# Writing down the order of ScalarE and VectorE, with weight slices between evacuations, in a retention and feed-forward kernel

## The chip, the cores and the metric

The kernel runs on one core of a Trainium2 chip. The metric is the device time of one execution in microseconds (us), as a median of several. Before the change it was 657.52 us (3 runs, 657.5 to 659.73). A difference counts as real here from 2% on; smaller ones are told with their intervals. All runs in this text are correct and in the fast state.

## The reference, cut to what matters

```python
# q, k, v: (4, 8, 768, 64) float32; w_in: 512 x 2048; w_out: 2048 x 512, both float64 by promotion
for t in range(S):                                     # retention, one state per head
    state = gamma * state + outer(k[t], v[t])
    y[t] = scale * q[t] @ state
x = y.transpose(0, 2, 1, 3).reshape(3072, 512)
h = x @ w_in                                           # 3072 x 2048
g = h * (1 / (1 + exp(-h)))                            # silu
return (g @ w_out).astype(float32)                     # 3072 x 512
```

## The kernel before

The sequence is cut into six chunks of 128 steps. A chunk c and a batch b make a *unit*, 24 in all; the four units of a chunk make *group* c, whose 512 rows of x go through w_in in 16 *products* (c, f), f being a slice of 128 columns. One unit's piece of attention is a *visit* (3.1 us of TensorE). When all 96 products are done, an output phase multiplies the stored g by w_out, a chunk of four output blocks at a time.

The weights arrive as float64. `convert_w` makes float32 out of them, one slice at a time, with one ScalarE operation (the absolute value `ca`) and six VectorE operations, the first two of them a sign and a clamp. `split_w` then makes three parts of the slice for three matrix passes. It is a chain across two engines: ScalarE high, VectorE low, then ScalarE middle and VectorE third.

```python
def split_w(f, w32, name, factor):
    w = w_slot(f, name)
    lo = conv.tile([128, 512], FP32, tag="wl", name=f"{name}l_{f}")
    with tc.issue_after(held[0] if f >= NF - 4 else evac[0]):
        nc.scalar.activation(out=w[:, 0, :], in_=w32, func=AF.Copy, scale=HALF * factor)
    high = w[:, 0, :].bitcast(FP32)
    nc.vector.scalar_tensor_tensor(out=lo, in0=w32, scalar=factor, in1=high, ...)
    nc.scalar.activation(out=w[:, 1, :], in_=lo, func=AF.Copy, scale=1.0 / EPS)
    nc.vector.scalar_tensor_tensor(out=w[:, 2, :], in0=high, scalar=EPS, in1=lo, ...)
    return w
```

A product is 12 matmuls into two of three banks (tiles of PSUM, the memory that TensorE writes), then an evacuation on ScalarE (a copy out of the first bank), a subtraction on VectorE (called g below; it reads the second bank) and the silu on ScalarE:

```python
def product_in(c, f):
    ha, hb = turn(f"ha_{c}_{f}"), turn(f"hb_{c}_{f}")          # two of three banks
    for i in range(3):
        for kk in range(KIN):
            nc.tensor.matmul(hb if i == 2 else ha, lhsT=w_sb[f][:, i, ts(kk, 128)], ...)
    nc.scalar.activation(out=hs, in_=ha, func=AF.Copy, scale=ONE_E)
    taken_out[:] = [nc.vector.tensor_tensor(out=hs, in0=hs, in1=hb, op=ALU.subtract).ins]
    nc.scalar.activation(out=hs, in_=hs, func=AF.Silu)
```

The order of TensorE is as written: after the first visits come eight products of two groups by turns (the *pairs*), twelve of three groups (the *threes*), then (2, 4) to (2, 11) and the rest. That of ScalarE and VectorE is the scheduler's, helped by `issue_after`:

```python
ctx.enter_context(tc.manual_schedule(engines={mybir.EngineType.PE}))
```

Group 2's x first lies in the place of the last four slices of w_in. It is therefore also stored, and read back into another place (`late_x`, the *readback*) before the products (2, 12) to (2, 15). g here and below is also the name of a product's result, the silu of h. The output phase ends each chunk with four blocks, in both kernels in the same words:

```python
for b in range(B):
    ...
    nc.scalar.activation(out=o, in_=oa, func=AF.Copy, scale=ONE_E)
    nc.vector.tensor_tensor(out=o, in0=o, in1=ob, op=ALU.subtract)
    nc.scalar.dma_start(out=out[ds(b * S + c * C, C), :], in_=o)
```

## Time and profile before

| Quantity | Before |
|---|---|
| Time | 657.52 us |
| Span in the profile | 655.4 us |
| TensorE (PE) busy | 617.1 us, 94% |
| VectorE (DVE) busy | 428.5 us, 65% |
| ScalarE (ACT) busy | 288.1 us, 44% |
| Last product done | about 388 us |

TensorE is the bound over the whole: 94% of the span. The two dearest groups of matmuls of the products, in the list of costliest groups, show it (line, engine, operation, tiles, shapes and count; then busy us and the mean ns of one; then idle time of the engine before them and what ended most of it):

```profile
L485 PE MATMUL ha<-xt,wi 128*128 128x512 f32 x768 | 194.2, 395 | 6.0 <-DVE g L490 4.3
L485 PE MATMUL hb<-xt,wi 128*128 128x512 f32 x384 | 103.0, 390 | 1.2 <-ACT g L489 1.1
```

In front of these 1152 matmuls there are 7.2 us of idle time in all: 4.3 us waiting for VectorE's subtraction g, 1.1 us for ScalarE's evacuation.

### The profile page before, as it was taken

The numbers are of one execution on the slowest core, as the hardware profiler recorded it, in microseconds if no ns is written. First come the engines' busy times: TensorE is split into PE (matmuls) and PEld (weight loads), VectorE is DVE, ScalarE is ACT, GpSimd is POOL, SyncE is SP. The second block draws the span as 40 slices with busy tenths as digits, with TensorE's granted clock in tenths as the row PEclk, the third lists the DMA queues.
The fourth block names the chain that finished last, engine by engine and source line by source line (L and its number), as shares of the span: only waits on it lengthen the run. The fifth ranks groups of instructions, "written<-read, shape, count | busy, mean of one in ns | idle before, by whom it ended". The sixth has DMA issues, their size and how long they took to land.

```text
span 655.4 us, 13531 instructions
## 1 busy us (share of the span) xinstructions
PE 617.1 (94%) x5440; PEld 509.2 (78%) x5440; DVE 428.5 (65%) x736; ACT 288.1 (44%) x522; POOL 14.9 (2%) x94
## 2 busy tenths in 40 slices
PE   4788889999999899999989999999999999999996
PEld 3676777888877687888768888888888888888885
DVE  2898989967968867658948856545463645454631
ACT  4546566756645444454437972222231412222311
POOL 3100000000000000000000000000000000000000
PEclk9998989999999999999999999999999999999999
DMA  9996775553577866767736654343242433433301
GB/s 196 211 209 153 198 199 179 185 171 127 192 242 170 235 178 162 226 170 237 240 113 225 202 169 127 100 159 101 92 163 95 147 110 98 159 99 95 129 0 64
DMA packets 123070, 103.64 MB, mean 158 GB/s; under 512 B 80000, under 2 KB 88192, under 8 KB 123008
## 3 DMA queue, kind: packets, MB, share of 16 engines
q1 hardware_dynamic: 119552, 96.49, 50.9%
q10 hardware_dynamic: 3456, 6.29, 2.6%
q8 instruction: 42, 0.69, 0.5%
q14 instruction: 20, 0.16, 0.1%
HBM read 66.06 MB, written 36.70 MB: 157 GB/s over the span
## 4 chain that ended last, share of the span: by engine, by line
PE 70%; DVE 17%; ACT 4%; DMA 3%; issue 3%; SPq 2%; ACTq 0%; DVEq 0%; POOL 0%; POOLq 0%
PE ha L485 18%; PE hb L485 9%; PE ob L612 7%; PE o L610 7%; PE oa L610 7%; PE o L611 7%; PE o L612 7%; PE oa L611 7%; SPq L144 2%; DVE cp L203 2%; DVE g L490 2%; DVE xt L433 2%; DVE cs L199 2%; PE y L387 1%; DVE am L363 1%
## 5 line engine op out<-in xcount | busy, mean ns | idle before, releaser
L485 PE MATMUL ha<-xt,wi 128*128 128x512 f32 x768 | 194.2, 395 | 6.0 <-DVE g L490 4.3
L485 PEld LDWEIGHTS ha<-xt,wi 128*128 128x128 f32 x768 | 142.6, 188 | 40.3 <-DVE g L490 8.3
L536 DVE TENSOR_TENSOR gs<-gr,gs 128x512 fp32r<-128x512 f32 x96 | 62.1, 685 | 90.3 <-ACT gs L534 90.3
L534 ACT ACTIVATE gs<-gr 128x512 fp32r<-128x512 f32 x96 | 53.5, 621 | 134.2 <-issue 131.8
L485 PE MATMUL hb<-xt,wi 128*128 128x512 f32 x384 | 103.0, 390 | 1.2 <-ACT g L489 1.1
L491 ACT ACTIVATE g<-g 128x512 f32<-128x512 f32 x96 | 60.6, 631 | 78.4 <-DVE g L490 78.2
L490 DVE TENSOR_TENSOR g<-g,hb 128x512 f32<-128x512 f32 x96 | 65.5, 682 | 44.4 <-PE hb L485 33.8
L485 PEld LDWEIGHTS hb<-xt,wi 128*128 128x128 f32 x384 | 71.9, 188 | 17.1 <-ACT g L489 1.6
L612 PE MATMUL ob<-wo,gs 128*128 128x512 f32 x192 | 75.3, 392 | 0.0
L610 PE MATMUL o<-wo,gs 128*128 128x512 f32 x192 | 74.7, 389 | 0.0
L610 PE MATMUL oa<-wo,gs 128*128 128x512 f32 x192 | 74.7, 389 | 0.0
L611 PE MATMUL o<-wo,gs 128*128 128x512 f32 x192 | 74.7, 389 | 0.0
L612 PE MATMUL o<-wo,gs 128*128 128x512 f32 x192 | 74.7, 389 | 0.0
L611 PE MATMUL oa<-wo,gs 128*128 128x512 f32 x192 | 74.7, 389 | 0.0
L489 ACT ACTIVATE g<-ha 128x512 f32<-128x512 f32 x96 | 56.6, 590 | 24.9 <-PE ha L485 20.1
L537 DVE SCALAR_TENSOR_TENSOR gs<-gs 128x512 fp32r<-128x512 f32 x96 | 61.9, 682 | 0.0
L612 PEld LDWEIGHTS ob<-wo,gs 128*128 128x128 f32 x192 | 36.0, 188 | 8.8 <-DVE o L618 1.5
L611 PEld LDWEIGHTS o<-wo,gs 128*128 128x128 f32 x192 | 36.0, 188 | 7.5
L612 PEld LDWEIGHTS o<-wo,gs 128*128 128x128 f32 x192 | 36.0, 188 | 7.5
L610 PEld LDWEIGHTS oa<-wo,gs 128*128 128x128 f32 x192 | 36.0, 188 | 7.5
L611 PEld LDWEIGHTS oa<-wo,gs 128*128 128x128 f32 x192 | 36.0, 188 | 7.5
L610 PEld LDWEIGHTS o<-wo,gs 128*128 128x128 f32 x192 | 36.0, 188 | 7.3
(80 smaller groups left out, 653.7 us busy)
## 6 DMA issues: line engine op xcount, KB each, us to landing
gd<-g SPq DMA_DIRECT2D x96, 256.0 KB, 2.9
gr<-gd SPq DMA_DIRECT2D x96, 256.0 KB, 2.7
wf<-in_moe_w_out_dram SPq DMA_DIRECT2D x16, 512.0 KB, 4.2
out_dram<-o ACTq DMA_DIRECT2D x24, 256.0 KB, 2.1
wf<-in_moe_w_in_dram SPq DMA_DIRECT2D x16, 256.0 KB, 3.2
wf<-in_moe_w_in_dram SPq DMA_DIRECT2D x32, 128.0 KB, 3.8
kf<-in_k_dram SPq DMA_DIRECT2D x16, 256.0 KB, 5.1
qf<-in_q_dram SPq DMA_DIRECT2D x16, 256.0 KB, 4.4
```

Of the source, the lines that this page charges most:

```text
L144: nc.sync.dma_start(out=t, in_=src[b, :, ds(c * C, C)].rearrange("h t d -> t h d"))
L199: nc.vector.scalar_tensor_tensor(out=s, in0=a, scalar=3, in1=s, op0=ALU.logical_shift_left, op1=ALU.bitwise_or)
L485: nc.tensor.matmul(hb if i == 2 else ha, lhsT=w_sb[f][:, i, ts(kk, 128)], rhs=xt[c][:, i, kk, :], start=kk == 0 and i != 1, stop=kk == KIN ...
L489: nc.scalar.activation(out=hs, in_=ha, func=AF.Copy, scale=ONE_E)
L490: taken_out[:] = [nc.vector.tensor_tensor(out=hs, in0=hs, in1=hb, op=ALU.subtract).ins]
L491: nc.scalar.activation(out=hs, in_=hs, func=AF.Silu)
L534: nc.scalar.activation(out=t[:, 0, :], in_=g, func=AF.Copy, scale=HALF)
L536: nc.vector.tensor_tensor(out=t[:, 1, :], in0=g, in1=high, op=ALU.subtract)
L537: nc.vector.scalar_tensor_tensor(out=t[:, 2, :], in0=t[:, 1, :].bitcast(FP32), scalar=-1.0 / EPS, in1=high, op0=ALU.mult, op1=ALU.add)
L610: nc.tensor.matmul(oa, lhsT=gh, rhs=wo[f][:, 0, :], start=first_, stop=False)
L611: nc.tensor.matmul(oa, lhsT=glo, rhs=wo[f][:, 1, :], start=False, stop=last)
L612: nc.tensor.matmul(ob, lhsT=gm, rhs=wo[f][:, 2, :], start=first_, stop=last)
```

## The change

Its intent is to take the order of ScalarE and VectorE from the scheduler and write it down: the conversion of weights becomes a generator that hands out single operations, and about 2000 ns of them are put in front of each product's evacuation, so that VectorE is always busy while TensorE multiplies. Two products, (1, 10) and (1, 11), are also moved behind (0, 12) to (0, 15), so that six products and not four are left to cover the readback of group 2's x. The diff, cut to its core ("..." marks cuts, here and below; comments in the diffs are added):

```diff
-    def split_w(f, w32, name, factor):
+    LONG, SHORT = 600, 360
+    def split_w(f, w32, name, factor, between=()):
         w = w_slot(f, name)
+        nc.scalar.activation(out=w[:, 0, :], in_=w32, func=AF.Copy, scale=HALF * factor)
+        yield from between                      # the next slice's absolute value, sign, clamp
         lo = conv.tile([128, 512], FP32, tag="wl", name=f"{name}l_{f}")
-        with tc.issue_after(held[0] if f >= NF - 4 else evac[0]):
-            nc.scalar.activation(out=w[:, 0, :], in_=w32, func=AF.Copy, scale=HALF * factor)
 ...
+        yield LONG
         nc.scalar.activation(out=w[:, 1, :], in_=lo, func=AF.Copy, scale=1.0 / EPS)
 ...
+    def fill(time):
+        while fillers and time > 0:
+            cost = next(fillers[0], None)
 ...
+                time -= cost
 ...
-    def product_in(c, f):
+    def product_in(c, f, time):
+        need(f + 1)
 ...
+        fill(time - catch_up())
         nc.scalar.activation(out=hs, in_=ha, func=AF.Copy, scale=ONE_E)
-        taken_out[:] = [nc.vector.tensor_tensor(out=hs, in0=hs, in1=hb, op=ALU.subtract).ins]
+        nc.vector.tensor_tensor(out=hs, in0=hs, in1=hb, op=ALU.subtract)
 ...
-    ctx.enter_context(tc.manual_schedule(engines={mybir.EngineType.PE}))
+    ctx.enter_context(tc.manual_schedule(engines={E.PE, E.Activation, E.DVE}))
 ...
+    half, full = NF // 2, 2000
 ...
+    steps += [(0, f) for f in early_f] + [(1, f) for f in early_f[:2]]
+    steps += [(0, f) for f in late_f] + [(1, f) for f in early_f[2:]]
 ...
+    here = steps.index((1, early_f[2]))
+    loads_at = {steps[here + b]: b for b in range(B)}
+    splits_at = {steps[here + 1 + b]: b for b in range(B)}
 ...
             if f < NF - 4:
-                w_out(f)
+                fillers.append(w_out(f))        # in group 5: before the evacuation, not after
+        product_in(c, f, full)
```

## The prediction

> **What bounds the kernel now.** I first cut the span where the program changes its work, with the view that sums each engine's busy time over stretches. Columns: stretch, its length, then busy time and instruction count of TensorE, weight load, VectorE, ScalarE, GpSimd, then granted clock, DMA share, GB/s.
>
> ```profile
> 55.00:104.00 49.00, 43.33 (x668) 36.06 (x665) 44.46 (x82) 28.87 (x51) 1.87 (x9) 0.95 0.71 192
> 104.00:153.30 49.30, 49.30 (x218) 40.77 (x218) 37.53 (x66) 31.74 (x56) 0.00 (x0) 1.00 0.51 168
> 153.30:257.10 103.80, 97.28 (x1152) 79.92 (x1150) 81.97 (x147) 54.70 (x94) 2.11 (x13) 1.00 0.66 193
> 257.10:344.50 87.40, 84.20 (x961) 68.67 (x962) 60.79 (x108) 41.03 (x72) 2.10 (x13) 1.00 0.61 194
> 344.50:388.00 43.50, 43.50 (x194) 36.02 (x193) 31.68 (x49) 33.97 (x60) 0.00 (x0) 1.00 0.63 200
> 388.00:655.40 267.40, 262.21 (x1153) 215.66 (x1151) 133.69 (x217) 69.24 (x125) 0.00 (x0) 1.00 0.34 110
> ```
>
> From 104 us on TensorE is nearly solid; only 55 to 104 is VectorE's (44.5 of 49 us). Idle TensorE time between 153 and 344 us is 6.5 + 3.2 = 9.7 us: about all that a better order there can win. The rest, 388 to 655 us, the change leaves alone.
>
> A product of 12 matmuls takes 2.72 us when dense (the first pieces of two products start 2.72 us apart: 106.77, 109.49). The rule that couples it to VectorE is in the order of time of both engines around 103 us (start, duration, instruction, idle time before it):
>
> ```profile
> 103.19 0.68 DVE L490 TENSOR_TENSOR g<-g,hb 128x512 f32<-128x512 f32 x1
> 103.78 0.68 DVE L118 SCALAR_TENSOR_TENSOR wil<-cs,wi 128x512 f32<-128x512 f32 x1
> 104.50 0.69 DVE L121 SCALAR_TENSOR_TENSOR wi<-wi,wil 128x512 fp32r<-128x512 f32 x1
> 105.11 0.68 DVE L490 TENSOR_TENSOR g<-g,hb 128x512 f32<-128x512 f32 x1
> ```
> ```profile
> 103.92 2.11 PE L485 MATMUL ha<-xt,wi 128*128 128x512 f32 x8 [0.65 <-DVE g L490]
> ```
>
> Three PSUM banks serve two per product, so product n+2 starts only when the subtraction g of product n is done: TensorE's start at 103.92 follows the end at 103.87. VectorE may therefore fall one product behind and no more. The same lines give rates: a long VectorE operation takes 0.60 us from start to start (0.33 for a short one, as in the start of 107.96 and the 108.30 after it), and 0.12 more when the next reads its result (103.78 to 104.50).
>
> The last view is that of waits, and one case of it in order of time on ScalarE:
>
> ```profile
> DVE ca L196 <- ACT ca L192: 14.1, 13, 1.4
> ```
> ```profile
> 206.91 0.63 ACT L491 ACTIVATE g<-g 128x512 f32<-128x512 f32 x1 [1.14 <-DVE g L490]
> 207.45 0.57 ACT L331 COPY qt<-qp 128x512 f32<-128x512 f32 x1
> 207.92 0.67 ACT L192 ACTIVATE ca<-wf 128x512 f32<-128x512 f32 x1
> ```
>
> ScalarE goes through its list in order: silu, then a copy, then the absolute value that VectorE's clamp needs, which so began only at 208.62 after 1.13 us idle. Such waits cost 1.1 us each (14.1/13).
>
> **What the Trainium skill says.** "PSUM — Partial Sum Buffer", section "Engine vs sequencer instructions": the queues of ScalarE, VectorE and GpSimd are strict FIFO. The trace agrees (lines above), and everything below rests on it. "Perfetto Trace Analysis", section "Optimizing Scalar/DVE Operations": a profiled duration is longer than what an instruction costs, because its write acknowledgement overlaps the next instruction. It agrees in kind (0.68 long, 0.60 apart), not in its "about twice"; I use the intervals.
>
> **The change part by part.** No arithmetic is added. Now VectorE and ScalarE run in written order, and at each product about 2000 ns (nominal: 600 a long operation, 360 a short one) of weight conversion stand in front of the product's own evacuation. I compared the built instruction lists of both kernels.
>
> *Products 2 to 19 in order, up to g(1,7).* In the new list VectorE has 89 long, 38 short and 37 dependent neighbours between g(0,0) and g(1,7): 89x0.60 + 38x0.33 + 37x0.12 = 70.4 us (63.2 in the old list: conversion is taken earlier). Within the twelve products of the second part it is 3.0 to 3.2 us a product against TensorE's 2.72: VectorE sets the pace. To this come waits for ScalarE. A w_in slice now has, after its last add: ScalarE high (0.60), ScalarE absolute value of the next slice (0.67), and on VectorE only one short operation before the clamp. That is 0.60+0.67+0.05-0.33 = 1.0 us idle per slice; 1.6 where it comes directly behind a silu or delays the evacuation, 1.5 to 2.0 where two transposes' copies stand before it too. Going through the list: 6.1 us in the pairs, 6.1 in the threes. Weights start later but the first g should end at about 61 (60.5 now). So g(0,7) ends at 61 + 68.5 + 12.2 = 142; product (2,3) then ends at 144.4, and eight products (2,4) to (2,11), with no conversion allowed in them, at 144.4 + 8x2.72 = 166. Now it is 153.3: **+13**. Those eight leave VectorE empty: the conversion was done too early, and TensorE paid.
>
> *(2,11) to g(3,6).* The four last w_in and all w_out slices are packed in here: 120 long, 73 short, 68 dependent = 104.3 us, plus 4.5 for the first product, whose slice waits for the end of (2,11). TensorE alone needs 26 products x 2.72 + 6 visits x 3.1 = 89. Waits for ScalarE's absolute value: about 7 us. The readback of x for group 2 now lies behind six products, which hides the loads better, but each of its four splits starts on ScalarE behind a silu that waits for VectorE, and its three loads after the first wait for a buffer whose product must be stored first (load and store 2.8 and 2.9 us each): 2 us each on VectorE, 8 in all. Sum 4.5 + 104.3 + 15 = 124 against 103.8: **+20**.
>
> *g(3,6) to the end of (4,15).* No conversion is left. 24 products x 2.72 + 4 visits x 3.1 + 2 x 2.2 = 82, with small waits 83.5 against 87.4: **-4**.
>
> *Group 5, f = 0 to 11.* The old order on ScalarE is the evacuation, high, silu, the middle part:
>
> ```profile
> 369.70 0.58 ACT L489 ACTIVATE g<-ha 128x512 f32<-128x512 f32 x1
> 370.18 0.62 ACT L116 ACTIVATE wo<-wr 128x512 fp32r<-128x512 f32 x1
> 371.04 0.63 ACT L491 ACTIVATE g<-g 128x512 f32<-128x512 f32 x1 [0.24 <-DVE g L490]
> 371.64 0.63 ACT L120 ACTIVATE wo<-wol 128x512 fp32r<-128x512 f32 x1
> ```
>
> The evacuation goes first, and the period is 2.5 us. In the new list ScalarE has high(f), middle(f), evacuation(f), silu(f); VectorE has wol, wo, g. Each needs the one before on the other engine: high 0.63, wol 0.68, middle 0.54, evacuation 0.58, g 0.68, silu 0.60, with four hand-overs of 0.04 = 3.87 us a product. It can't shrink through slack, for high(f) writes over the weights of product f and so waits for its end. Time to the end of the evacuation of f=11 and 0.95 of matmuls after it: 11x3.87 + 3.5 = 46 instead of 12x2.72 = 32.6: **+13.5**.
>
> Sum: +13 + 20 - 4 + 13.5 = +42.5, 657.5 to 700. The ScalarE waits were added as if VectorE were always late; some will coincide. I take off 5: **695 us**.
>
> **Rivals.** *The order works as meant:* its author's budget is 2000 + 600 = 2600 ns, under the product's 2720. For it: old TensorE idle time of 9.7 us after 153 and VectorE gaps before 104. Against: the generator overshoots (an average list of 2200 nominal), and dependent neighbours cost 0.12. With no wait for ScalarE at all: -1 before (2,11), 109-104 = +5, -4: about 657 if group 5 is free as well.
> *Only group 5 hurts:* 657 + 13.5 = 671. For it: that chain is the surest step. Against: the 14.1 us of clamp waits in the old trace, where the order was kinder.
> *Stores become the wait:* cw shares one buffer with wol, and a store of it already held VectorE for 2.40 us once; if each of 15 costs 0.5, 700 + 8 = 708.
>
> **Range and chances.** 672 is the second rival with a little more; 714 is the full sum with the third and a further 6. To be faster by 2% it would need 644.4, which means 13 us out of 9.7 of idle TensorE plus what the start gives: 0.01. Within 2% (to 670.7) needs all ScalarE waits hidden: 0.06. Slower: 0.93.
>
> **What would show it.** Right: in group 5, g starts every 3.9 us and TensorE waits for the evacuation and for g; waits of the clamp for the absolute value grow from 14 to 25 us or more; waits of ha for g from 4.3 to tens of us; (2,11) ends near 166, g(3,6) near 290; VectorE's total of busy time hardly moves; VectorE is almost empty from 144 to 166 and in group 4. Wrong: group 5 dense at 2.72 (then in-order evacuation is no limit), or products in the threes spaced 2.72 us (then VectorE's intervals are shorter than I took).

## The result, and the profile after

The changed kernel took 725.19 us (4 runs, 723.15 to 725.32) against 658.62 us (4 runs) of the kernel before beside it: ratio 1.1002, 95% interval 1.0968 to 1.1036. A ratio here is always the mean time of one kernel's runs over that of the other's of the same rounds, so not quite the ratio of the medians quoted. All outputs are right. The span of the profiled run is 723.3 us. The direction was right; 725 lies outside the range of 672 to 714.

The same 96 subtractions g follow each other on VectorE in both kernels, so their count cuts the span in comparable stages. The 28th belongs to product (2, 11), the 55th to (3, 6), the 80th to (4, 15) and the last to (5, 15). The table gives the end in us of the n-th g, and the length of the stage that it closes:

| Stage, closed by | Before, end | After, end | Before, length | After, length | Difference |
|---|---|---|---|---|---|
| start, 1st g | 60.5 | 63.4 | 60.5 | 63.4 | +2.9 |
| 28th g | 154.0 | 171.8 | 93.5 | 108.4 | +14.9 |
| 55th g | 257.1 | 302.9 | 103.1 | 131.1 | +28.0 |
| 80th g | 345.4 | 387.1 | 88.3 | 84.2 | -4.1 |
| 96th g | 388.9 | 444.6 | 43.5 | 57.5 | +14.0 |
| output phase, end of span | 655.4 | 723.3 | 266.5 | 278.7 | +12.2 |

The differences sum to 67.9 us. The view that sums busy time over stretches shows the same of the changed kernel (columns as in the prediction; the stretches end about where the stages do):

```profile
111.00:171.00 60.00, 53.15 (x217) 41.31 (x218) 36.67 (x63) 30.93 (x53) 0.00 (x0) 0.97 0.40 135
171.00:303.00 132.00, 109.83 (x1153) 85.13 (x1152) 110.81 (x200) 57.22 (x104) 2.52 (x13) 0.92 0.66 200
303.00:386.40 83.40, 82.81 (x962) 69.17 (x963) 35.48 (x56) 37.92 (x64) 2.11 (x13) 1.00 0.42 131
386.40:443.90 57.50, 48.25 (x198) 36.02 (x197) 30.25 (x45) 33.06 (x58) 0.00 (x0) 1.00 0.42 134
443.90:723.30 279.40, 267.02 (x1147) 213.30 (x1146) 146.16 (x222) 70.94 (x127) 0.00 (x0) 1.00 0.37 108
```

In 171 to 303 VectorE is busy for 110.8 us and TensorE is idle for 22; directly after it VectorE is busy for only 35.5 of 83.4 us. The conversion is packed into one stage and missing from the next. The granted TensorE clock is 0.92 in 171 to 303, against 1.00 before in 153 to 257, and the same matmuls are busy for 109.8 us instead of 97.3. That rival does not set the stage's length: between 171.1 and 302.9 us no idle time of VectorE above 0.15 us is put down to TensorE. Group 5 has 9.3 us of idle TensorE where before it had none. The last line is the surprise: 12.4 us of idle time in the output phase, against 5.2 before.

The two groups of matmuls shown before, in the list of costliest groups of the changed kernel:

```profile
L540 PE MATMUL ha<-xt,wi 128*128 128x512 f32 x768 | 201.2, 405 | 10.3 <-DVE g L546 8.4
L540 PE MATMUL hb<-xt,wi 128*128 128x512 f32 x384 | 111.1, 413 | 29.5 <-ACT g L545 29.5
```

The wait of hb for the evacuation grew from 1.1 to 29.5 us: work put in front of an in-order evacuation is seen on TensorE as a wait for the evacuation, not for the work.

The reason that it is hb is in the banks, as the code hands them out. The second bank of a product (hb) is the one that the first (ha) of the product before it had, so it needs that product's evacuation. Only the ha of the product after that needs g.

**Group 5.** In order of time on ScalarE (start, duration, instruction, and in brackets the idle time before it and what ended it):

```profile
401.85 0.63 ACT L126 ACTIVATE wo<-wol 128x512 fp32r<-128x512 f32 x1 [0.76 <-DVE wol L123]
402.39 0.58 ACT L545 ACTIVATE g<-ha 128x512 f32<-128x512 f32 x1
403.72 0.63 ACT L547 ACTIVATE g<-g 128x512 f32<-128x512 f32 x1 [0.75 <-DVE g L546]
404.26 0.63 ACT L119 ACTIVATE wo<-wr 128x512 fp32r<-128x512 f32 x1
405.64 0.63 ACT L126 ACTIVATE wo<-wol 128x512 fp32r<-128x512 f32 x1 [0.76 <-DVE wol L123]
```

The loop goes high (404.26), middle (405.64), evacuation, silu, with a wait for VectorE in front of middle and of silu. It closes in 3.79 us (401.85 to 405.64), against 2.72 us of matmuls in a product.

**The output phase.** The end of a chunk's products on ScalarE, first of the kernel before (ACTq are issues of transfers by its sequencer), then of the changed one:

```profile
429.67 1.28 ACT L617 ACTIVATE o<-o 128x512 f32<-128x512 f32 x2 [6.59 <-PE o L612]
430.84 0.59 ACT L617 ACTIVATE o<-oa 128x512 f32<-128x512 f32 x1
431.02 1.61 ACTq L619 DMA_DIRECT2D out_dram<-o  x3
432.68 0.60 ACT L617 ACTIVATE o<-oa 128x512 f32<-128x512 f32 x1 [1.25 <-DVE o L618]
```

```profile
486.16 0.60 ACT L676 ACTIVATE o<-o 128x512 f32<-128x512 f32 x1 [1.17 <-PE oa L670]
487.51 0.34 ACTq L678 DMA_DIRECT2D out_dram<-o  x1
487.89 0.60 ACT L676 ACTIVATE o<-oa 128x512 f32<-128x512 f32 x1 [1.14 <-DVE o L677]
489.24 0.34 ACTq L678 DMA_DIRECT2D out_dram<-o  x1
489.63 0.60 ACT L676 ACTIVATE o<-oa 128x512 f32<-128x512 f32 x1 [1.14 <-DVE o L677]
```

The scheduler had put three evacuations in front of the first three stores. In written order each store stands between two evacuations, and a store waits for VectorE's subtraction of its block. So the next evacuation waits too: 1.74 us from one to the next (487.89 to 489.63), although it needs nothing from that subtraction. TensorE wants a bank back every 0.68 us there (three matmuls at 0.227), and from the timeline of TensorE at this chunk's end (486.68 to 491.34) ten steps that take 2.27 us when dense took 4.66: 2.4 us lost, at five changes of chunk 12 us (an estimate from this one).

**Smaller things.** One line of TensorE before its first product, then two of VectorE in the stage of the readback:

```profile
52.33 1.12 PE L368 MATMUL kp<-ident,kf 128*128 128x128 f32 x4 [3.11 <-DMA kf<-in_k_dram]
```

```profile
212.93 0.69 DVE L224 TENSOR_TENSOR cw<-cs,cp 128x512 f32<-128x512 f32 x1 [2.02 <-DMA wod<-cw]
...
218.60 0.69 DVE L472 TENSOR_TENSOR xt<-yr,xt 128x512 fp32r<-128x512 f32 x1 [3.58 <-ACT xt L469]
```

TensorE waited 3.1 us for k of unit 9, whose load stood in SyncE's queue behind the load of a weight slice that waited for its place. VectorE waited 3.6 us for one split of the reread x, and 2.0 us for the store of a converted slice whose buffer it wanted.

### The profile page after: what moved, and what is told of

Same layout as the page of the kernel before. It is cut to its first block, busy times and chain, and to the rows that moved or that the text cites. A ratio compares the mean times of both kernels' runs of the same rounds, so it can differ in the third digit from the quotient of the medians.

```text
span 723.3 us, 13553 instructions
## 1 busy us (share of the span) xinstructions
PE 645.7 (89%) x5440; PEld 515.6 (71%) x5440; DVE 445.4 (62%) x736; ACT 287.7 (40%) x522; POOL 15.4 (2%) x94
## 4 chain that ended last, share of the span: by engine, by line
PE 61%; DVE 16%; ACT 8%; issue 5%; DMA 4%; SPq 4%; ACTq 1%; DVEq 0%; POOLq 0%; POOL 0%
PE ha L540 13%; PE hb L540 9%; PE oa L669 6%; PE ob L671 6%; PE o L671 6%; PE o L669 6%; PE oa L670 6%; PE o L670 6%; SPq L151 3%; DVE g L546 3%; PE y L424 2%; ACT o L676 2%; ACT g L545 2%; DVE o L677 2%; ACT ca L198 1%
## 5 line engine op out<-in xcount | busy, mean ns | idle before, releaser
L540 PE MATMUL ha<-xt,wi 128*128 128x512 f32 x768 | 201.2, 405 | 10.3 <-DVE g L546 8.4
L540 PEld LDWEIGHTS ha<-xt,wi 128*128 128x128 f32 x768 | 146.5, 194 | 48.4 <-DVE g L546 14.5
L540 PE MATMUL hb<-xt,wi 128*128 128x512 f32 x384 | 111.1, 413 | 29.5 <-ACT g L545 29.5
L592 DVE TENSOR_TENSOR gs<-gr,gs 128x512 fp32r<-128x512 f32 x96 | 65.9, 686 | 72.9 <-ACT gs L590 72.9
L593 DVE SCALAR_TENSOR_TENSOR gs<-gs 128x512 fp32r<-128x512 f32 x96 | 66.4, 692 | 3.3
```

The costliest lines, as they stand in the source:

```text
L592: nc.vector.tensor_tensor(out=t[:, 1, :], in0=g, in1=high, op=ALU.subtract)
L593: nc.vector.scalar_tensor_tensor(out=t[:, 2, :], in0=t[:, 1, :].bitcast(FP32), scalar=-1.0 / EPS, in1=high, op0=ALU.mult, op1=ALU.add)
```

## The experiments

Twelve kernels ran, in three calls of four (e1, e2, e3, e6; then e4, e5, e7, e8; then the rest, on another chip); those of one call shared a chip and the runs of the kernel before, whose medians in the three calls lay at 658 us within 0.1. In the call of the changed kernel it was 658.62, so a saving quoted against the changed kernel's 725.19 is good to about 1 us. My theory after the result: four separate orderings cost the time and add up, namely the pace of 2000 ns, the row stores, group 5's order, and the absolute value that comes too late. The rival: VectorE is simply full, and mending one place moves the loss to the next.

### e1_rows_last

Changed kernel, with the stores of a chunk behind all four of its evacuations.

```diff
+        rows = []
 ...
-            nc.scalar.dma_start(out=out[ds(b * S + c * C, C), :], in_=o)
+            rows.append((b, o))
+        for b, o in rows:
+            nc.scalar.dma_start(out=out[ds(b * S + c * C, C), :], in_=o)
```

> The changed kernel, but at the end of each of the six output groups ScalarE first evacuates all four row blocks and only then issues their four stores. Theory (in the written order each store stands in ScalarE's list between two evacuations, waits there for VectorE's subtraction, and holds the next evacuation: 1.74 us a block in the trace instead of about 0.6): the stretch from the first output product to the end shrinks from 279 to about 268 us, total 725 - 11 = 714 us. Rival (the tail grew because the splits of the next group, or the loads of g, come later): no change, 722 to 727 us.

Measured: 710.84 us, ratio 1.0802 (1.0773 to 1.0830), 14.3 us less than the changed kernel, three more than expected. The stretch of the output phase:

```profile
443.90:708.50 264.60, 259.92 (x1147) 214.77 (x1145) 144.91 (x221) 70.31 (x127) 0.00 (x0) 1.00 0.39 114
```

All stages before it end within 0.3 us of the changed kernel's. The whole loss of the output phase was the place of four stores a chunk that the diff does not touch. The phase is even shorter than before (264.2 against 266.5 us from the 96th g). Of these 2.3 us, 0.5 come after the start of the last matmul (5.61 to 5.12 us), where the last chunk's four stores now leave without the pause in front of the fourth; the rest comes before it.

### e2_group5

Changed kernel; group 5 evacuates first and lets the weights' chain run around the subtraction.

```diff
-                fillers.append(w_out(f))
+                inside[c, f] = w_out(f)
 ...
         nc.vector.tensor_tensor(out=hs, in0=hs, in1=hb, op=ALU.subtract)
+        w = inside.pop((c, f), None)
+        if w:
+            next(w)                 # high, low
         nc.scalar.activation(out=hs, in_=hs, func=AF.Silu)
+        for _ in w or ():
+            pass                    # middle, third
```

> The changed kernel, but in group 5 the order of a product is evacuation, g, high, wol, silu, middle, wo instead of high, wol, middle, wo, evacuation, g, silu. Theory (a chain that goes back and forth between ScalarE and VectorE and holds the evacuation: 3.80 us a product in the trace): g comes every 2.72 us in group 5, total 725 - 13.5 = 711.5 us. Rival (VectorE's or the DMA's load, which stays the same, sets the 3.80 us): less than 4 us gained, over 721 us.

Measured: 712.45 us, ratio 1.0835 (1.0797 to 1.0874), 12.7 us less. Three lines of ScalarE of that run:

```profile
401.99 0.58 ACT L545 ACTIVATE g<-ha 128x512 f32<-128x512 f32 x1
402.75 0.63 ACT L119 ACTIVATE wo<-wr 128x512 fp32r<-128x512 f32 x1 [0.18 <-PE hb L540]
403.54 0.63 ACT L550 ACTIVATE g<-g 128x512 f32<-128x512 f32 x1
```

Evacuation, high, silu, middle: each operation fills the wait of another, g comes every 2.72 us, and the stage takes 44.5 us with TensorE busy for all of it. The chain across the engines was the limit, as the prediction had it.

### e3_abs_early

Changed kernel; the absolute value of slice i+1 is issued two VectorE operations earlier, in the middle of converting slice i and ahead of ScalarE's high.

```diff
         yield SHORT
+        if i + 1 < 2 * NF:
+            early_abs(i + 1)
         nc.vector.scalar_tensor_tensor(out=p.bitcast(FP32), in0=lo, scalar=2.0 ** -52, ...)
```

> The changed kernel, but ScalarE takes the absolute value of slice i+1 two VectorE operations before the last add of slice i, not behind the high part of slice i. Same operations. Theory (VectorE is the pace in the pairs, in the threes and up to g(3,6), and its waits for the absolute value lie on the path): these waits fall from 14.9 us to under 4, total 725 - 13 = 712 us (708 to 717). Rival (VectorE has slack there, the waits are hidden): 722 to 727 us.

Measured: 715.49 us, ratio 1.0873 (1.0823 to 1.0924), 9.7 us less. Waits of the clamp for the absolute value, 14.9 us in the changed kernel, are gone from its list of waits. About two thirds of them came back as time: 6 us by the 28th g (165.6 against 171.8) and 5 more by the 55th, where 11.2 us of it are had; a little is lost again later.

### e6_pace

Changed kernel, with one number changed.

```diff
-    half, full = NF // 2, 2000
+    half, full = NF // 2, 1400
```

> The changed kernel with one number changed: 1400 instead of 2000 nominal ns of conversion in front of a product. Theory (the conversion is pushed in faster than VectorE can take it beside the subtractions, 3.0 to 3.2 us a product plus waits against TensorE's 2.72, and eight products and group 4 then have none): 2.25 to 2.5 us plus waits a product, (2,11) ends near 156 instead of 171, group 3 and 4 together lose some of it again; total 725 - 38 = 687 us (680 to 697). Rival (total work on VectorE and the order on ScalarE set the time, not the pace): 715 us or more.

Measured: 695.86 us, ratio 1.0576 (1.0547 to 1.0605), 29.3 us less: the largest of the four, though short of the 38 hoped for. Its stretches from the 28th to the 55th and from there to the 80th g:

```profile
158.60:270.40 111.80, 101.32 (x1149) 79.22 (x1147) 89.89 (x163) 53.81 (x97) 2.30 (x13) 0.98 0.66 194
270.40:357.10 86.70, 84.59 (x965) 69.59 (x966) 55.70 (x96) 40.30 (x71) 2.10 (x13) 1.00 0.57 180
```

VectorE's 110.8 us became 89.9, and 35.5 became 55.7: the same work, 20 us of it moved to where VectorE had room. The first of these stages became 19.3 us shorter and the second 2.4 longer; the stage before them, up to the 28th g, became 12.4 shorter (96.0 against 108.4). So VectorE was not full over the span; it was full where the number put the work.

### e4_pe_only

Changed kernel with all its program order, but only TensorE's order fixed; the scheduler arranges the other two again.

```diff
-    ctx.enter_context(tc.manual_schedule(engines={E.PE, E.Activation, E.DVE}))
+    ctx.enter_context(tc.manual_schedule(engines={E.PE}))
```

> The changed kernel, but only TensorE keeps the written order, as in the kernel before; ScalarE and VectorE are ordered by the scheduler again. The six products, the single operations and the new order of products stay. Theory (the written order of ScalarE and VectorE is the cause): back to within 10 us of the kernel before, 650 to 668 us. Rival (the new order of products, or the pace at which conversions are issued, costs by itself): over 685 us.

Measured: 667.66 us, ratio 1.0155 (1.0118 to 1.0191), 57.5 us less and just inside what was expected, at its upper end. Six sevenths of the loss come from fixing the order of two engines; under the scheduler, the new program order costs only the rest. That rest lies mostly in the stage from the 28th to the 55th g, 112.4 us against 103.1; group 5 (43.5) and the output phase (266.5) are as before.

### e5_pe_dve

The same, with VectorE's order fixed as well and only ScalarE's left to the scheduler.

```diff
+    ctx.enter_context(tc.manual_schedule(engines={E.PE, E.DVE}))
```

> The changed kernel, but ScalarE alone is ordered by the scheduler; TensorE and VectorE keep the written order. Theory (what ScalarE's order holds is 14 in the tail, 13 in group 5 and some 13 to 20 of waits for the absolute value and at the readback; VectorE's pace stays): 725 - 45 = 680 us (672 to 690). Rival 1 (VectorE's written order is the cause and ScalarE only follows): over 705 us. Rival 2 (ScalarE's order is all of it): under 666 us.

Measured: 686.25 us, ratio 1.0439 (1.0399 to 1.0480), in the expected range. Undone in this order, ScalarE's order is worth 38.9 of the 57.5 us (725.2 to 686.3) and VectorE's the other 18.6 (686.3 to 667.7). So undone, the engine that is busy 40% of the time did more harm than the one at 62%. The opposite order, VectorE freed and ScalarE fixed, was not run, so the shares are not shown to be independent of it.

### e7_six_alone

Kernel before, with only the two products moved, so that six cover the readback.

```diff
-            [(c, f) for c in range(2) for f in range(half, NF - 4)])
-    last = [(c, f) for c in range(3) for f in range(NF - 4, NF)]
+            [(0, f) for f in range(half, NF - 4)] + [(1, half), (1, half + 1)])
+    last = ([(0, f) for f in range(NF - 4, NF)] + [(1, half + 2), (1, half + 3)] +
+            [(c, f) for c in (1, 2) for f in range(NF - 4, NF)])
 ...
-    for i, bs in enumerate(((0, 1), (2,), (3,))):
-        behind[1, NF - 4 + i] = lambda bs=bs: [late_x(b) for b in bs]
+    for b, x in enumerate(((1, half + 2), (1, half + 3), (1, NF - 4), (1, NF - 3))):
+        behind[x] = lambda b=b: late_x(b)
```

> The kernel before with one part of the change alone: its scheduler keeps ScalarE and VectorE, but the products (1,10) and (1,11) come after (0,12) to (0,15), and the four readbacks of x of group 2 are each behind one of (1,10) to (1,13), so six products lie over them and not four. Theory (the readback's visible stall before, 1.3 us of idle TensorE at 188 to 195 us and part of the 1.0 us before the next visits, goes): 1 to 4 us faster than before, 0.994 to 0.998. Rival (the loads wait for the buffers of hs whose products must be stored first, wherever they stand): same, 0.998 to 1.002.

Measured: 661.28 us, ratio 1.0061 (1.0032 to 1.0089): a miss for both sides, a little slower where one said a little faster and the other the same. The six products hide nothing by themselves: the stage with the readback, from the 28th to the 55th g, is 103.2 us against 103.1. What was lost lies after it, from the 55th to the 80th g (91.6 against 88.3), part of it at a granted clock of 0.98 against 1.00; the cause is not known.

### e8_four_mends

e1, e2, e3 and e6 together, on the changed kernel.

> The changed kernel with four edits together: stores after all four evacuations, evacuation first in group 5, absolute value early, 1400 instead of 2000. Theory (four separate causes in different stretches, only the absolute value and the pace overlap): 725 - 14 - 13 - 29 - 4 = 665 us (656 to 671), so still a little slower than before. Rival (they share one cause, for example the clock or the DMA load): over 680 us.

Measured: 656.86 us, ratio 0.9981 (0.9953 to 1.0008), at the lower end of what was expected. The four alone saved 14.3 + 12.7 + 9.7 + 29.3 = 66.0 us; together they saved 68.3 (725.2 to 656.9). They add up, so the rival falls: no loss moved to the next place, and the 4 us of overlap that the theory took off did not show. With them the written order is as good as the scheduler's, not better.

### e9_readback

e8, with the loads of x of group 2 issued one product earlier.

```diff
-    loads_at = {steps[here + b]: b for b in range(B)}
+    loads_at = {steps[here - 1 + b]: b for b in range(B)}
```

> The kernel with the four mends (656.9 us), and group 2's x is loaded back one product earlier, its splitting left where it is. Theory: in the four-mends kernel the readback still costs PE about 6 us in five waits between 185 and 205 us, because the load stands in SyncE's queue behind a weight slice's load that waits for its place, and ScalarE and VectorE, in written order, wait for it at the head of their lists. One product of 4.8 us earlier should hide most of that: 652 us, 650 to 655; the longest wait of xt's copy on the load falls from about 2 us to under 1. Rival: the time goes to the splits themselves (1.3 us of each engine per turn among evacuations) and the load is no matter: 656 or more. Second rival: the four loaded tiles share the buffers of g, so earlier loads hold g's buffers and PE waits there instead: 656 or more with waits on g's tiles.

Measured: 653.12 us, ratio 0.9928 (0.9905 to 0.9952), inside the theory's range. The wait of VectorE for ScalarE's part of a split of x, in the lists of waits of e8 and then of this run (us in total, times, longest):

```profile
DVE xt L478 <- ACT xt L475: 11.4, 6, 4.4
```

```profile
DVE xt L478 <- ACT xt L475: 6.9, 5, 2.1
```

Of these, the four waits for the reread x fell from 8.8 to 4.9 us, and ScalarE's waits for the loads (3.6 us in e8) are gone from the list. In the two profiled runs the stage with the readback is 1.6 us shorter, though the medians differ by 3.7. This run suggests that the moved products pay only once the loads go ahead of them; earlier loads without the moved products were not tried. It is the best, 0.7% faster than the kernel before and so still "the same" by the 2% rule (e13 and e14 do not differ from it by more than their intervals). Of the 2.5 us between the spans of the two profiled runs (655.4 and 652.9), 2.3 lie in the output phase (266.5 to 264.2, from the 96th g on) and 0.2 before it. In these two runs what beats the kernel before therefore lies where the place of the stores acts; the rest of the new order only draws level. The stores were not tried on the kernel before itself.

### e13_early_kqv

e9, with the loads of k and q of units 8 and 9 and of v of unit 8 at the very start.

> The readback edit of the run before in this batch, and the loads of k and q of units 8 and 9 and of v of unit 8 put behind the first eight units' loads at the start, where nothing stands before them that waits for a buffer. Theory: the 3.4 us in which PE waited at 53 us for k of unit 9, queued behind a weight slice's load that waits for its place, go: 3 us less than the run with the readback edit alone, so 649 us, 646 to 652, and no wait of PE on a load of k outside the first 12 us. Rival: VectorE and ScalarE are behind by then anyway (PE waits 2.1 us for ScalarE at 47 us and for g in the first products), so the wait comes back as one for them: under 1 us less.

Measured: 653.99 us, ratio 0.9946 (0.9919 to 0.9973), no better than e9: the rival was right. TensorE's wait for k is gone from the list of waits (2.5 us in e9), and another took its place; first e9, then this run:

```profile
PE kp L374 <- DMA kf<-in_k_dram: 2.5, 1, 2.5
```

```profile
PE y L432 <- ACT ys L466: 7.4, 4, 3.6
```

In e9 the wait for that ScalarE copy of y was 3.5 us in 3 times. So taking away this one wait was not enough.

### e14_pace_1200 and e15_pace_1700

e13, with 1200 and with 1700 in place of 1400.

> The kernel with early k and q loads, and 1200 instead of 1400 for the work put in front of each evacuation. Theory: at 1400 the pairs and threes put about as much VectorE work between two evacuations as two products of PE hide, so a lower pace gains nothing more and only moves conversions to later groups: within 4 us of the run at 1400. Rival: VectorE's work per product is still the bound of the first 300 us, and the gain goes on at the slope that 2000 to 1400 showed (29.3 us for 600, so 9.8 us for 200): 640 us.

> The kernel with early k and q loads, and 1700 instead of 1400. Theory: half of the way back to 2000, and if the cost goes in proportion to the work above what the products hide, half of the 29.3 us: 13 to 16 us more than the run at 1400. Rival: the cost sets in only near 2000, where a whole conversion falls before one evacuation: under 6 us more.

Measured: 653.48 us (ratio 0.9930, 0.9907 to 0.9954) and 669.26 us (1.0174, 1.0148 to 1.0200). At 1200 nothing more is won; 300 above 1400 cost 15.3 us, half of the 29.3 us that 600 cost. Both numbers fit the theories and not the rivals, but the stages tell more. At 1200 TensorE waits 7.6 us for weight slices that come too late (wi), which it does not do at 1400, while its waits for the evacuation fall from 5.2 to 0.3 us: one wait is traded for another. At 1700, 13.0 us of the loss lie between the 28th and the 55th g and 1.9 before, while from 1400 to 2000 (e6) it was 19.3 and 12.4; e6 and e15 also start from different kernels. A loss in proportion to the surplus work therefore fits the totals, and is not shown for the single stages.

## Why the prediction was right or wrong

**Right: the pace in kind, and group 5.** VectorE's pace and its waits for ScalarE did hold TensorE up to (3, 6), as e6 and e3 show. For group 5 the prediction had a closed chain of 3.87 us a product and +13.5; it was 3.79 and +14.0, and e2 takes it away by its order alone. (The old period of 2.5 us was read from one pair of evacuations; over the stage it is 43.5/16 = 2.72.) For the stage after (3, 6) it had 83.5 us in place of 87.4; it took 83.4. Its sign that VectorE is almost empty held for the eight products without conversion (4.5 us busy in 149 to 166), not for group 4 and the end of group 3 (35.5 of 83.4 us).

**Too loose: "VectorE may therefore fall one product behind and no more".** The rule follows only the bank that g frees. The waits of ha for g were to grow from 4.3 us to tens; they became 8.4. The wait that grew was that of hb for the evacuation, 1.1 to 29.5 us. It has less room: between the end of a product's matmuls and the hb of the next lie only that one's eight ha matmuls, 1.8 us at 0.227 each, and not a whole product of 2.72.

**The step that failed: "The rest, 388 to 655 us, the change leaves alone."** No term and no rival of the prediction stands for that phase, and the diff hardly touches it. Fixing the order on ScalarE fixes it for the whole program, the output phase included, where the scheduler had moved three stores behind three evacuations. In written order the phase took 12.3 us longer, and e1 shows that the place of the stores is all of it. Without that loss the time lies inside the predicted range: e1 took 710.84 us. With the term added, the best guess would have been 707, still 18 us short; the rest is below.

**Mis-sized: the stage to (2, 11), +13.** It became +17.7 (the end of (2, 11) on TensorE: 153.3 to 171.0). Of the 4.7 us, 2.4 came before the first g, which ended at 63.4 and not at 61; TensorE's 3.1 us wait for k of unit 9 lies there, which the prediction did not see, though in e13, on a mended kernel, taking that wait away won nothing. The other 2.3 us in the pairs and threes were not traced to one cause.

**Mis-sized: (2, 11) to (3, 6), +20.** It became +28. The prediction's waits were about right in size: 7 us for the absolute value (6.6 measured in that stretch, 1.4 of it within the first product), 8 for the readback (7.4). The first product, set at 4.5 us, took 5.5 (171.0 to 176.5). Two more terms were short. VectorE's operations after that were set at 104.3 us from start to start; without the waits that the profile names they took 109.5 in the trace. Of these 5.2 us, by estimate 1.6 are six operations too many counted as short (the trace has 126 long and 67 short, the prediction 120 and 73), and 1.4 the 0.08 us more that each of the 17 operations with such a wait behind it shows; the rest is not explained. And the stores of converted slices, which the sum had left to the third rival, held VectorE for 3.8 us in four places.

**Wrong: "I take off 5".** The waits were assumed to coincide partly with time in which VectorE would have stood idle anyway. In (2, 11) to (3, 6), after 171.1 us, no wait of VectorE is put down to TensorE, so every wait for ScalarE or a store lengthened the stage, and the four mends add up (66.0 us apart, 68.3 together).

**A sign that failed: "waits of the clamp for the absolute value grow from 14 to 25 us or more".** They stayed at 14.9 us in all. In the changed kernel's list of waits:

```profile
DVE ca L203 <- ACT ca L198: 14.9, 17, 1.8
```

Before, of these 14.1 us 3.2 fell up to the 28th g, 5.1 up to the 55th and 5.9 up to the 80th; now they are 8.3, 6.6 and none. They have moved into the stages that VectorE paces, and e3 won 9.7 us. A wait's total says little of its price; the stage it falls in does.

**Another: VectorE's total was to "hardly move".** It rose from 428.5 to 445.4 us with the same 736 instructions, 12.5 of the 16.9 in the output phase (133.7 to 146.2). Where an operation does not read the one in front of it, it starts before that one ends in the profile, and the overlap counts once. Counted in the traces, 505 operations overlap so with the next one before and 317 after. Two pieces of a split of g in the output phase, first of the kernel before (x2: the same step on two tiles), then of the changed one (the two steps of one tile, 0.72 us apart):

```profile
443.49 1.29 DVE L536 TENSOR_TENSOR gs<-gr,gs 128x512 fp32r<-128x512 f32 x2 [4.67 <-ACT gs L534]
```

```profile
494.69 0.69 DVE L592 TENSOR_TENSOR gs<-gr,gs 128x512 fp32r<-128x512 f32 x1
495.41 0.69 DVE L593 SCALAR_TENSOR_TENSOR gs<-gs 128x512 fp32r<-128x512 f32 x1
```

The differences add up: 4.7 and 8 for the two stages, 0.4 for the next two, 5 that should not have been taken off, 12.3 for the output phase, together 30.4, which is what lies between the predicted 37.5 (42.5 - 5) and the 67.9 of the spans.

Still open: why the new program order costs about 10 us under the scheduler (e4), and why the two moved products alone cost 3 to 4 us (e7).

## What to carry to other kernels

Fixing an engine's order in this way fixes it in every phase, also in code that the diff does not touch; compare the instruction lists of all phases, and look first for transfers issued by a computing engine between two evacuations. Put evacuations ahead of fill-in work, run a chain that crosses engines in the waits of another chain, and give each slot less fill-in than the products hide: here 1400 nominal ns beside a 2.72 us product cost no more than 1200, and each 100 more cost about 5 us in total. The four mends of the in-order lists added up here, so measuring them one at a time told what they were worth together.

## What the Trainium skill lacked or had wrong

- "PSUM — Partial Sum Buffer", section "Engine vs sequencer instructions", has the queues of ScalarE and VectorE as strict FIFO. That held, but the section does not say that an issue of a transfer in ScalarE's list holds the computing instructions behind it while it waits for its data: 1.14 us idle and 1.74 us a block here. "Perfetto Trace Analysis", section "Per-instruction lifecycle: what the profiler-reported window actually captures", does draw the wait on the issuing sequencer, without a price for the instructions behind it.
- "DMA: Bandwidth & Descriptors", section "Issuing engines are not separate DMA queues", says that issuing from several engines saves only the sequencer's time, usually small beside the transfer. The issue itself was indeed small (0.34 us on ScalarE), but the issuing engine's place in line was worth 14.3 us (e1).
- "VectorE: DVE Perf Modes", section "The DRAIN you can't avoid", measured that a semaphore after each of eight copies costs nothing extra; it has no number for an operation that reads its neighbour's result. Here an operation that reads its neighbour's result started 0.72 us after it (103.78 to 104.50 in the kernel before), an independent one 0.60. Whether the wait or the pipeline takes the 0.12 us, no run here tells.
- "Perfetto Trace Analysis", section "Optimizing Scalar/DVE Operations", gives VectorE on SBUF an overhead of about 60 ns an instruction, and profiled about twice that, which leaves some 60 ns between profile and cost. Here it was a little more, 0.08 us (0.68 long, 0.60 between starts).
- No page tells that the order alone moves an engine's busy time: VectorE's 736 instructions took 428.5 us in one order and 445.4 in the other, with 505 and 317 of them overlapping the next.
